# A long-convolution kernel: where two loads stand in the SyncE queue of an even step

## The chip, the cores and the metric

The kernel runs on one core of one Trainium2 chip. The metric is the device time of one execution in microseconds (us), as the median of several runs. A second source is one profiled execution, which gives every instruction of every engine with its start and its duration.

## The reference

Two blocks are computed one after the other, in float32. The first convolves 8 sequences of 5696 x 128 with one filter of the same length, by a Fourier transform of doubled length. The second is a soft mixture of experts over all 45568 resulting rows.

```python
Xf = np.fft.rfft(x, n=2 * S, axis=1)              # x: (8, 5696, 128)
Hf = np.fft.rfft(h, n=2 * S, axis=0)              # h: (5696, 128)
y = np.fft.irfft(Xf * Hf[None], n=2 * S, axis=1)[:, :S, :]
x = y.reshape(8 * 5696, 128)
logits = x @ phi                                  # 32 slots
d = softmax(logits, axis=0)                       # over the rows
slot_input = d.T @ x
slot_out = relu(slot_input @ w1[e]) @ w2[e]       # 4 slots for each of 8 experts
out = softmax(logits, axis=1) @ slot_out
```

## The kernel before, in words

The transform is split in two factors, N1 = 90 and N2 = 64, and is done for nine "batches": the filter h first (batch 0), then the eight sequences. The work of a batch is cut into 8 chunks (NJ = 8), and a hand-written loop over steps `t` (line 631) runs a software pipeline: one step starts one chunk of a batch, and later stages of earlier batches run in the same step. An even and an odd step make a pair. Nothing reorders the work: each engine does its instructions in the order in which the program writes them.

**The stages.** `stage_a(t, ...)` is the first factor (L241, TensorE), for the lower 60 of 90 frequencies in every step and for the upper 30 of two chunks in every odd step. ScalarE moves its result to `fst` (L243), and the SyncE queue stores it to the DRAM tensor `f` (L225): two stores of 240 KB for the lower frequencies, four of 120 KB for the upper ones. A batch's spectra are complete when its eight steps are over. They come back as tiles `gt`, one for each of 12 "units" of a batch, by `load_g` (L270, 512 KB). `stage_b1(u)` is the second factor on unit u and the product with the filter (L284 on TensorE into `bt`, L304 and L312 on VectorE). `stage_b2(u)` is the first factor of the inverse (L327 into `bz`); ScalarE moves it to `zst` (L332), and SyncE stores it: units 0 to 7 to `zm` in two stores of 256 KB, units 8 to 11 to `zr` in four stores of 128 KB (32 KB in the last unit). The frequencies in `zr` are z's last ones. `stage_c1(T)` is the last factor for a pair of chunks, T: matmuls L412 on `zc` (loaded from `zm`, `load_main`, L374, 1024 KB) and then L417 on `zx` (loaded from `zr`, `load_rest`, L385, 512 KB). It runs at the head of an odd step. All else (logits, the two softmaxes, the dispatch) follows on its result in later steps.

**Who does what where.** A step of a multiple of eight (t = 8, 16, ... 72) is the first in which a batch's spectra may be loaded. `prefetch(last)` issues `load_g` for units up to `last`, as far as their batch is stored. It is called from `slot_b` behind each `stage_b1(u)` with `u + AHEAD`, AHEAD = 3. There are three `gt` buffers, so `load_g(u)` can start when `stage_b1(u - 3)` is over. The first unit of a new batch is multiplied in the odd step that follows, behind `stage_c1`.

Steps t = 26, 34, ... 74 precede a new batch's first `stage_c1` (T = 0, 4, ... 24). In these the line `load_rest(pair(-1))` (L694) loads `zx` for that T. For the other three T of a batch, both loads stand together in an odd step, two steps ahead of their use (L680 to L682). There is a single pair of `zc` and `zx` buffers.

**The SyncE queue.** Nearly all transfers are issued by SyncE in program order. `pending` holds stores that are written down but not yet issued; `flush()` issues them. Each issue uses one of eight semaphores in turn, and first waits until the DMA that used it eight issues before has landed. `load_x` (L198) loads the input of a later chunk (768 KB).

In program order, an even step issues this on SyncE before the change:

| | t = 32, 40, ... 64 | t = 34, 42, ... 66 |
|---|---|---|
| 1 | `load_x` | `load_rest` (zx) |
| 2 | two stores of `f` | `load_x` |
| 3 | `load_g` of units 0 and 1 | two stores of `f` |
| 4 | stores of `zr` | `load_g` |
| 5 | `c_t`, `load_g` of unit 2, stores of `zr` | two stores of `zm` |
| 6 | | `c_t`, `load_g`, two stores of `zm` |

Of the kernel before, what the change touches and what calls it, by code (L numbers as in the profile page):

```python
# [70 lines left out]
def kernel(  # L71
# [34 lines left out]
    NJ = HALF // CH  # L106
# [6 lines left out]
    NQ = NJ // 2  # L113
# [95 lines left out]
    def fold(c):  # L209
        if c not in xs:  # L210
            return
        t_ = xs.pop(c)
        y_ = xf[c % len(xf)]
        i = CH * (c % 2)
        near, far = t_[:, 0, i:i + CH, :], t_[:, 1, ::-1, :][:, i:i + CH, :]
        for o in range(2):
            nc.gpsimd.tensor_tensor(out=y_[:, o, :, :], in0=near, in1=far,  # L217
                                    op=AL.subtract if o else AL.add)
        folded[c] = y_
# [3 lines left out]
    def flush():  # L223
        while pending:
            pending.pop(0)()  # L225
# [4 lines left out]
    def stage_a(c, high):  # L230

        g, j = divmod(c, NJ)
        st = apool.tile([P, CH, 2, D], F32, name="fst", tag="fst", bufs=4)
        if high:
            groups = [(c_, o, HALF, slice(HP, HP + HALF)) for c_ in (c - 1, c) for o in range(2)]
        else:
            groups = [(c, o, HP, slice(0, HP)) for o in range(2)]
        for q in range(2):
            p = bank()
            for i, (c_, o, m, cols) in enumerate(groups):  # L240
                nc.tensor.matmul(p[i * m:(i + 1) * m, :], s1[:, g // B, q + o, cols], columns(c_, o),  # L241
                                 start=True, stop=True)
            nc.scalar.activation(st[:, :, q, :],  # L243
                                 p[:, :].rearrange("p (n d) -> p n d", d=D), AF.Copy)
        k0, k1 = (LOW, N1) if high else (0, LOW)
        for i, (c_, o, m, _) in enumerate(groups):
            n0 = o * HALF + CH * (c_ % NJ)
            pending.append(partial(
                nc.sync.dma_start,
                out=fd[g][k0:k1, n0:n0 + CH, :, :].rearrange("k n c d -> k (n c d)"),  # L250
                in_=st[i * m:i * m + k1 - k0, :, :, :].rearrange("k n c d -> k (n c d)")))
        if high:
            for c_ in (c - 1, c):
                del folded[c_]
# [9 lines left out]
    def load_g(u):  # L264
        if u >= (B + 1) * NW:
            return
        g, w, us = parts(u)
        n = sum(k for _, k in us)
        t_ = bpool.tile([P, 4, 2, D], F32, name="gt", tag="gt", bufs=3)
        nc.sync.dma_start(  # L270
            out=t_[:, 0:n, :, :].rearrange("p q c d -> p q (c d)"),
            in_=fd[g][8 * w:8 * w + 2 * n].rearrange("(q a) r c d -> (a r) q (c d)", a=2))
        gs[u] = t_
# [42 lines left out]
    def stage_b2(u):  # L316
        g, w, us = parts(u)
        if g == 0:
            return
        m = len(us)  # L320
        y_ = prods.pop(u)
        bz = bps.tile([P, 2, 2, 2 * D], F32, name="bz", tag="bz")
        for o, (i, n) in enumerate(us):
            for q in range(n):
                r = slice(q * HP, (q + 1) * HP)
                for a in range(2):
                    nc.tensor.matmul(bz[a * HP:(a + 1) * HP, q, o, :], vt[r, i, a, :],  # L327
                                     y_[r, a * m + o, :, :].rearrange("p c d -> p (c d)"),
                                     start=True, stop=True)
        n = us[0][1]  # L330
        st = bpool.tile([P, 2, 2, 2 * D], F32, name="zst", tag="zst", bufs=3)
        nc.scalar.activation(st[:, 0:m, 0:n, :].rearrange("p o q x -> p q o x"),  # L332
                             bz[:, 0:n, 0:m, :], AF.Copy)
        k = m * n
        sv = st[:, :, :, :].rearrange("p o q x -> p (o q) x")
        for o in range(2):
            if 8 * w < MAIN:
                pending.append(partial(
                    nc.sync.dma_start,
                    out=zm[g - 1][o, 8 * w:8 * w + 2 * k].rearrange("(q a) r c d -> (a r) q (c d)", a=2),  # L340
                    in_=sv[o::2, 0:k, :]))
                continue
            k0 = 8 * w - MAIN
            for c in range(2):
                pending.append(partial(
                    nc.sync.dma_start,
                    out=zr[g % 2][o, c, k0:k0 + 2 * k].rearrange("(q a) r d -> (a r) q d", a=2),
                    in_=sv[o::2, 0:k, c * D:(c + 1) * D]))
# [30 lines left out]
    def load_rest(T):  # L379
        if T >= NT:  # L380
            return
        b, j = divmod(T, NQ)
        t_ = zs[T]
        n = 2 * CH
        nc.sync.dma_start(  # L385
            out=t_[1][:, :, :, :].rearrange("p h n d -> p (h n d)"),
            in_=zr[(b + 1) % 2].rearrange("o c k r d -> (o c k) r d")[:, j * n:(j + 1) * n].rearrange(
                "p r x -> p (r x)"))
# [214 lines left out]
    def units(t):  # L603
        g, i = divmod(t - LAG_B, NJ)
        if t < LAG_B or g > B:
            return []
        return [g * NW + k for k in range(sum(PER[:i]), sum(PER[:i + 1]))]
# [4 lines left out]
    AHEAD = 3  # L612
# [16 lines left out]
    wait_b2 = []  # L629

    for t in range(last_front + 1):
        us = list(units(t))

        def pair(lag):
            T, half = divmod(t - LAG_C - lag, 2)
            return T if half == 0 and 0 <= T < NT else None

        def prefetch(last):
            nonlocal loaded
            while loaded < len(queue) and queue[loaded][0] <= last \  # L640
                    and queue[loaded][0] // NW * NJ + NJ <= t:
                load_g(queue[loaded][0])
                loaded += 1

        def slot_b(due=True):
            fresh = due and bool(us)
            if fresh:
                u = us.pop(0)
                stage_b1(u)
                prefetch(u + AHEAD)  # L650
                wait_b2.append(u)
            if len(wait_b2) > fresh:
                stage_b2(wait_b2.pop(0))

        T, U, V, W, X = [pair(k) for k in (0, 2, 1, 3, 5)]
        if t < NA:
            stage_a(t, False)
            fold(t + 1)
        if t == last_front:
            assert T is None and U is None  # L660
            assert pair(-1) % NQ
            flush()
            dispatch(W)
            for i in range(3):
                slot_b()
                flush()
                if i == 1:
                    softmax_sum(W)
                    stage_c2(V)
            assert not us and not wait_b2  # L670
            stage_c6(X)
            stage_c3(V)
            column_max(V)
            break
        if t % 2:
            if T is not None:
                stage_c1(T)()
            flush()
            if pair(-2) is not None:
                load_main(pair(-2))  # L680
                if pair(-2) % NQ:
                    load_rest(pair(-2))  # L682
            slot_b()
            if U is not None:
                stage_c4(U)
            if t < NA:
                stage_a(t, True)
            if U is not None:
                stage_c5(U)
                softmax_exp(U)  # L690
            flush()
        else:
            if pair(-1) is not None and pair(-1) % NQ == 0:
                load_rest(pair(-1))  # L694
            if t < NA:
                load_x(t // 2 + 2)
            flush()
            if t == NJ:
                prefetch(AHEAD - 1)
            slot_b()  # L700
            if W is not None:
                softmax_sum(W)
                dispatch(W)
            flush()
            if V is not None:
                stage_c2(V)
            if X is not None:
                stage_c6(X)
            slot_b()
            if V is not None:  # L710
                stage_c3(V)
                column_max(V)
            flush()
        if t == NA:
            lead.close()
            wts = inner.enter_context(tc.tile_pool(name="wts", bufs=1, side="right"))
            w1s = wts.tile([P, E, F], F32, name="w1s")
        if NA < t <= NA + E:
            nc.sync.dma_start(out=w1s[:, t - NA - 1, :], in_=moe_w1[t - NA - 1])
# [213 lines left out]
```

## Time and profile before

| | |
|---|---|
| median of 3 runs | 912.35 us (912.24 to 916.9) |
| the profiled execution | 909.23 us, its span 907.4 us |
| mean granted TensorE clock | 0.903 |
| TensorE busy | 760.2 us (84% of the span) |
| VectorE, ScalarE, GpSimd busy | 601.4, 436.8, 399.8 us |
| DMA | 278.33 MB, mean 307 GB/s |

The profile's engines: PE is TensorE (matmuls), PEld its weight loads, DVE VectorE, ACT ScalarE, POOL GpSimd, SP SyncE, whose work is all issuing ("SPq"). "out<-in" names the tile written and the tiles read; L284 is line 284 of the kernel. Times count from the span's start. "PE bt L284 <- DMA gt<-f" reads: TensorE sat idle before the matmuls of L284 until a load of `gt` landed. When a DMA lands is seen from the trace's semaphore events, since each issue names its semaphore.

### The profile page before, as it was taken

How to read it: one execution, taken by the hardware profiler on the slowest of the kernel's cores; microseconds unless marked ns; L12 is line 12 of the kernel's file. 1: busy time of each engine (PE TensorE's matmuls, PEld its weight loads, DVE VectorE, ACT ScalarE, POOL GpSimd, SP SyncE). 2: the span in 40 equal slices, each digit the busy share in tenths (PEclk: the TensorE clock that was granted, in tenths of full speed). 3: DMA queues.
4: the chain of work that ended last, by engine and by line, in shares of the span. 5: the costliest groups of instructions: out<-in, count | busy, mean ns of one | idle time of the engine just before them, and what ended most of it. 6: DMA issues, size and time to landing. Idle time of an engine off the chain costs nothing.

```text
span 907.4 us, 21291 instructions
## 1 busy us (share of the span) xinstructions
PE 760.2 (84%) x8308; PEld 387.7 (43%) x8308; DVE 601.4 (66%) x896; ACT 436.8 (48%) x880; POOL 399.8 (44%) x353
## 2 busy tenths in 40 slices
PE   6857778689999989999998999799888877767893
PEld 2212233234444444444444444344444434344793
DVE  2029767568778867886877787678778766653552
ACT  2423234335556545665655655456544444563441
POOL 4634322444555655655655566456332224651000
PEclk9979889999999999999999999899988888766855
DMA  8989999999999999999999999999998768540798
GB/s 267 318 275 343 293 296 337 298 314 376 341 291 375 361 326 308 372 358 299 357 364 335 295 373 348 303 308 346 306 291 304 264 200 341 186 166 1 292 406 335
DMA packets 170443, 278.33 MB, mean 307 GB/s; under 512 B 13543, under 2 KB 128231, under 8 KB 165135
## 3 DMA queue, kind: packets, MB, share of 16 engines
q1 hardware_dynamic: 169336, 275.74, 89.7%
q10 hardware_dynamic: 1008, 1.25, 0.5%
q8 instruction: 66, 1.08, 0.5%
q14 instruction: 33, 0.27, 0.1%
HBM read 147.94 MB, written 129.00 MB: 305 GB/s over the span
## 4 chain that ended last, share of the span: by engine, by line
PE 47%; DMA 23%; ACT 8%; POOL 8%; DVE 6%; issue 6%; SPq 1%; ACTq 0%; DVEq 0%; POOLq 0%
PE bank L241 9%; DMA gt<-f 9%; PE bt L284 9%; PE bz L327 6%; POOL y L430 5%; PE bank L412 4%; DMA f<-fst 4%; PE op L886 3%; PE bank L439 3%; PE bank L417 3%; PE bank L448 2%; DMA zx<-zr 2%; ACT fst L243 2%; DMA out_dram<-o 2%; PE bank L527 2%
## 5 line engine op out<-in xcount | busy, mean ns | idle before, releaser
L241 PE MATMUL bank<-x,s 128*32 128x512 f32 (+1 forms) x1152 | 218.0, 620 | 12.9 <-POOL x L217 8.4
L217 POOL TENSOR_TENSOR x<-xc 128x512 f32<-128x512 f32 x144 | 180.4, 1278 | 107.2 <-PE bank L241 86.5
L284 PE MATMUL bt<-gt,wt 64*64 64x256 f32 x1620 | 125.0, 419 | 72.8 <-DMA gt<-f 33.0
L430 POOL TENSOR_TENSOR y<-y,op 128x512 f32<-128x512 f32 x64 | 77.6, 1213 | 206.8 <-DVE op L404 204.3
L304 DVE TENSOR_TENSOR pi<-bt,Hi 128x1024 f32<-128x1024 f32 x96 | 113.0, 1177 | 83.5 <-PE bt L284 83.3
L243 ACT ACTIVATE fst<-bank 128x512 f32<-128x512 f32 x216 | 122.8, 592 | 86.0 <-PE bank L241 57.7
L332 ACT ACTIVATE zst<-bz 128x1024 f32<-128x1024 f32 x96 | 93.3, 972 | 128.3 <-PE bz L327 109.4
L284 PEld LDWEIGHTS bt<-gt,wt 64*64 64x64 f32 x1620 | 58.3, 141 | 151.2 <-issue 79.1
L312 DVE TENSOR_TENSOR yf<-bt,pi 128x512 f32<-128x512 f32 x192 | 119.4, 663 | 3.3
L304 DVE TENSOR_TENSOR bt<-bt,Hr 128x1024 f32<-128x1024 f32 x96 | 113.0, 1177 | 0.0
L241 PEld LDWEIGHTS bank<-x,s 128*32 128x32 f32 (+1 forms) x1152 | 55.1, 126 | 129.8 <-issue 93.6
L327 PE MATMUL bz<-yf,vt 64*64 64x256 f32 x1440 | 110.4, 404 | 0.0
L327 PEld LDWEIGHTS bz<-yf,vt 64*64 64x64 f32 x1440 | 64.3, 143 | 25.5 <-issue 4.2
L512 POOL TENSOR_TENSOR L<-L,rs 128x512 f32<-128x512 f32 x32 | 33.5, 1048 | 91.6 <-DVE rs L511 66.4
L404 DVE TENSOR_TENSOR y<-bank,y 128x512 f32<-128x512 f32 x32 | 22.1, 692 | 76.7 <-ACT y L420 76.5
L439 PE MATMUL bank<-ident,y 109*128 109x109 f32 x512 | 62.7, 273 | 7.9 <-ACT yt L441 7.9
L504 ACT ACTIVATE L<-L 128x512 f32<-128x512 f32 x32 | 20.2, 630 | 94.7 <-POOL L L501 94.6
L430 POOL TENSOR_TENSOR y<-y,om 128x512 f32<-128x512 f32 x54 | 63.9, 1183 | 2.1
L439 PEld LDWEIGHTS bank<-ident,y 109*128 109x128 f32 x512 | 52.9, 149 | 19.4 <-POOL x L217 14.7
L412 PE MATMUL bank<-zc,im 64*64 64x512 f32 x480 | 60.8, 623 | 0.0
L441 ACT ACTIVATE yt<-bank 128x360 f32<-128x360 f32 x128 | 53.0, 482 | 7.7 <-PE bank L439 7.3
L420 ACT ACTIVATE y<-bank 128x512 f32<-128x512 f32 x32 | 19.1, 596 | 72.6 <-PE bank L417 72.6
(101 smaller groups left out, 862.5 us busy)
## 6 DMA issues: line engine op xcount, KB each, us to landing
gt<-f SPq DMA_DIRECT2D x99, 512.0 KB
f<-fst SPq DMA_DIRECT2D x144, 240.0 KB
zm<-zst SPq DMA_DIRECT2D x128, 256.0 KB
zc<-zm SPq DMA_DIRECT2D x30, 1024.0 KB
xc<-in_x_dram SPq DMA_DIRECT2D x32, 768.0 KB
f<-fst SPq DMA_DIRECT2D x144, 120.0 KB
out_dram<-o SPq DMA_DIRECT2D x16, 1024.0 KB
zx<-zr SPq DMA_DIRECT2D x30, 512.0 KB
```

Source lines behind the costliest of these rows:

```text
L217: nc.gpsimd.tensor_tensor(out=y_[:, o, :, :], in0=near, in1=far, op=AL.subtract if o else AL.add)
L241: nc.tensor.matmul(p[i * m:(i + 1) * m, :], s1[:, g // B, q + o, cols], columns(c_, o), start=True, stop=True)
L243: nc.scalar.activation(st[:, :, q, :], p[:, :].rearrange("p (n d) -> p n d", d=D), AF.Copy)
L284: nc.tensor.matmul(bt[q * HP:(q + 1) * HP, a, o, :], wt[r, 2 * i + q, :], t_[r, 2 * o + q, :, :].rearrange("p c d -> p (c d)"), start=True ...
L304: nc.vector.tensor_tensor(out=p_, in0=pv, in1=h_, op=AL.mult)
L312: nc.vector.tensor_tensor(out=y_[r, 0:k, c, :], in0=pv[:, :, c, :], in1=pi[r, 0:k, 1 - c, :], op=op_)
L327: nc.tensor.matmul(bz[a * HP:(a + 1) * HP, q, o, :], vt[r, i, a, :], y_[r, a * m + o, :, :].rearrange("p c d -> p (c d)"), start=True, sto ...
L332: nc.scalar.activation(st[:, 0:m, 0:n, :].rearrange("p o q x -> p q o x"), bz[:, 0:n, 0:m, :], AF.Copy)
L412: nc.tensor.matmul(ps[o, c][h_ * HP:(h_ + 1) * HP, :], im[r, c, :], zt[r, h_, :, c, :], start=True, stop=False)
L430: eng.tensor_tensor(out=part_, in0=part(v, 0), in1=o_[:, :, :], op=sign)
L439: nc.tensor.transpose(p[:, i * TR:(i + 1) * TR], ys[T][0:TR, k * CH + i, 0:D], ident[0:TR, 0:TR])
L441: nc.scalar.activation(yt[:, k * CH:(k + 1) * CH, :, :], of_tokens(p), AF.Copy)
```

## The change

In steps that are a multiple of 8, `prefetch` is called at the head of the step, ahead of `load_x` and of the stores of `f`. From t = 16 on, its limit is three units above the last multiplied one, so that it issues the new batch's first unit alone; unit 1 stays where it was. At t = 8, it issues units 0, 1 and 2. In steps 26, 34, ... 74, `load_rest` leaves the head of the step and stands behind the first `slot_b` and a `flush()`, hence behind `load_x`, the stores of `f`, the first `load_g` and the first two stores of `zm`.

```diff
         else:
-            if pair(-1) is not None and pair(-1) % NQ == 0:
-                load_rest(pair(-1))
+            if t % NJ == 0:
+                prefetch(wait_b2[-1] + AHEAD if wait_b2 else AHEAD - 1)
             if t < NA:
                 load_x(t // 2 + 2)
             flush()
-            if t == NJ:
-                prefetch(AHEAD - 1)
             slot_b()
+            if pair(-1) is not None and pair(-1) % NQ == 0:
+                flush()
+                load_rest(pair(-1))
             if W is not None:
                 softmax_sum(W)
                 dispatch(W)
```

## The prediction

> **What bounds the kernel now.** I read the page first, then the waits, the chain of waits, and the timeline at the two places that the change touches.
>
> ```profile
> span 907.4 us, 21291 instructions
> PE 760.2 (84%) x8308; PEld 387.7 (43%) x8308; DVE 601.4 (66%) x896; ACT 436.8 (48%) x880; POOL 399.8 (44%) x353
> ```
>
> PE is the busiest engine. In the middle of the span it is nearly the only bound: in the PE timeline the first-factor matmuls of odd steps start at 265.67, 285.82 and 305.97, so a pair of steps takes 20.15 us, and PE's gaps in two such pairs sum to 1.5 us. What PE loses there is lost to the span. The waits tell to whom it loses most:
>
> ```profile
> PE bt L284 <- DMA gt<-f: 33.0, 10, 10.2
> ```
>
> Eight of these ten are the first unit of a new batch: 10.2 us at t = 9, then 5.2, 3.1, 0.5, 3.4, 2.1, 1.7 and 5.5 at t = 17, 25, ... 65, and none at 73; together 31.6. The chain of waits shows the largest of the middle, and the other place that the change touches:
>
> ```profile
> 506.52 5.35 DMA zr<-zst
> 511.94 4.60 DMA zx<-zr
> 516.59 1.19 PE bank L417 x16
> ...
> 575.05 8.04 DMA gt<-f
> 583.22 1.99 PE bt L284 x16
> ```
>
> The columns are start and length. A load of `gt` is issued at 575.05, takes 8.04 us, and PE starts 0.1 us after it lands. But `zx` also lands at 516.54, and L417 starts at 516.59: that load has no slack. The SyncE timeline of step 34 shows what stands behind it:
>
> ```profile
> 265.26 0.35 SPq L385 DMA_DIRECT2D zx<-zr  x1
> 265.66 0.76 SPq L198 DMA_DIRECT2D xc<-in_x_dram  x1
> 266.46 0.88 SPq L225 DMA_DIRECT2D f<-fst  x2
> 267.44 0.41 SPq L270 DMA_DIRECT2D gt<-f  x1
> 267.95 1.83 SPq L225 DMA_DIRECT2D zm<-zst  x2
> ```
>
> and the PE timeline what waits for it:
>
> ```profile
> 267.53 1.95 PE L412 MATMUL bank<-zc,im 64*64 64x512 f32 x16
> 269.41 1.11 PE L417 MATMUL bank<-zx,ir 26*64 26x512 f32 x16
> ```
>
> By the semaphore events, this `zx` landed at 269.20, 3.9 us after its issue and 0.2 us before its use. The `gt` load issued two microseconds later landed at 274.98 (7.5 us), the second `zm` store at 276.28 (7.2 us). Most DMAs of this stretch land in the order of issue, about 1.4 us apart for 512 KB: they queue, and what stands ahead in the queue sets the landing.
>
> **Part 1, the first spectra.** Nothing is added or removed; one `load_g` (three at t = 8) passes `load_x` and two stores of `f`. At t = 32, `load_x` is issued at 242.00 and `gt` at 243.51, so the issue moves up 1.5 us. For the landing the bytes that it passes count. 512 KB of `gt` take 1.4 us between landings, so 768 KB of `load_x` take about 2.1, an estimate from that; the two stores of `f` land 0.6 to 0.7 us apart each. So the load lands some 3.4 us earlier. At t = 8 and 16 it cannot be issued earlier: it follows the lower stores of `f` of the step before, which land at 49.23 and 97.84, just when the load is issued now; but the transfers that it passes are still behind it, so I count the same there. The bound of this from below is nothing. Each wait shrinks by what it has, up to 3.4: 3.4 + 3.4 + 3.1 + 0.5 + 3.4 + 2.1 + 1.7 + 3.4 = 21.0 us. If the queue is also shorter by then, all but the 10.2 and the 5.2 go completely, 23.1.
>
> What was passed comes later: `load_x` and `f` by the time of one `gt`, 1.4 us. `load_x` feeds a fold three steps (30 us) later, and the stores of `f` are read eight steps on, so both are covered. ScalarE waits for a store of `fst` only in the first 105 us (27.6 us, 11 times); past that its four buffers cover the 1.4. At t = 8 three loads pass and stand waiting until 49.23, which puts `load_x` and `f` some 6 us back; PE's own 10.2 us wait hides that, and uncovered it would eat the 3.4. Unit 1 is next: at t = 32 it lands at 252.13 and is multiplied at 257.45, so it has 5 us of slack.
>
> **Part 2, z's last frequencies.** `load_rest` passes behind `load_x`, two `f`, one `gt` and two `zm`: 768 + 480 + 512 + 512 = 2272 KB on SyncE's only queue. It issues no new DMA. It adds a wait: SyncE now has to see the `zst` of that slot ready before `zx` goes; at t = 34 the two `zm` are issued at 267.95 with `zst` evicted at about 261.7, so that wait is covered. Taken away is SyncE's stop at the head of the step until the `zr` stores have landed, 0.2 to 0.8 us, with which `load_x` waited.
>
> Where will `zx` land? From above: the same seven transfers have to move, so it lands when the last of them does now. Those landings are 197.68, 276.28, 360.23, 442.13, 524.52, 609.75 and 681.62 for t = 26, 34, ... 74; L417 starts now at 190.13, 269.41, 353.20, 435.75, 516.59, 602.76 and 682.45. The differences are 7.6, 6.9, 7.0, 6.4, 7.9, 7.0 and none: 42.8 us. From below: issued when the second `zm` has been, less its own 0.4 us at the head, and taking only what it takes now at the head, 3.9 to 4.9 us; that gives 3.6, 3.9, 2.7, 2.5, 3.8 and 3.2, together 19.7. Nearest are `gt` and `zm` at that place in the queue, with 7.2 to 7.7 us, so I take the upper end, less the stop that is removed and the issue of `zx` itself (0.75 us in each of six): 38.3.
>
> L417 sits at the head of the odd step, and PE is in order: behind it are L284, L327 and the next first factor; ScalarE waits for it with the eviction (L420), then VectorE and GpSimd (L430). So PE stands still for the whole wait.
>
> The Trainium skill would make this smaller: "DMA: Bandwidth & Descriptors", in its section on the anatomy of one DMA, gives a fixed 2.0 us plus bytes over 436 GB/s (fitted on another issue path), which for 512 KB is an estimate of 3.2 us from issue to landing. By it, `zx` issued at 269.4 would land at 272.6, and the six waits would be some 3 us each and the whole change near zero. The 7.5 us of `gt` in the same place speaks against it here, since that rule knows no queue.
>
> **The clock.** A long wait costs more than itself. The windows view of the 5.5 us wait and after it, with PE's busy time first and the granted clock, DMA share and GB/s last:
>
> ```profile
> 577.71:583.22 5.51, 0.00 (x0) 0.03 (x1) 2.67 (x4) 1.09 (x2) 2.66 (x3) 0.74 1.05 358
> 583.22:587.00 3.78, 3.78 (x24) 2.09 (x24) 1.74 (x2) 0.38 (x1) 2.00 (x2) 0.50 1.03 334
> ```
>
> After it PE ran at half clock for 3.8 us. The eight steps with it (odd step 59 to 67, 512.56 to 599.02) took 86.5 us, against 80.5 for those with the 1.7 us wait (51 to 59): 5.9 more for 3.8 more of wait, so the clock cost 2.1. The same for the waits of 3.4 and 2.1 us (83.8 and 82.5 us) gives 1.6 each. Six new long waits at 2.1 are 12.6; those at t = 17, 41, 49 and 65 that shorten or go give back 1.6 x 3 + 2.1 = 6.9. Net +5.7 us. "TensorE: Matmul & The Clock Gate", on oscillation, puts the limit at PE idle for more than about 3.4 us; here 2.1 us sufficed at 416.4 (0.53 granted after it), 1.7 at 498.6 did not (1.00).
>
> **The sum.** 38.3 + 5.7 - 21.0 = +23 us. Against the profiled execution, 909.2 (907.4 of span and 1.8 around it), that is 932. The median of the runs lies 3.1 above that execution: 935.
>
> **The rivals.**
>
> *The saved waits do not count.* Between a batch's first unit and its `zx` there are ten microseconds. If the DMA queue does not move up with PE, PE reaches L417 earlier and waits longer for the same landing. Then the savings of t = 25 to 65 (14.2 us) are lost, and +37 remains, with the upper end of part 2 +42: 949 to 954. For it: DMA is at 358 and 334 GB/s around 583. Against it: SyncE waits for PE and ScalarE in the steps between, so its stream moves with them.
>
> *The load is cheap behind the stores.* `zx` takes what it takes now: 19.7, at most 6 x 1.6 - 6.9 = 2.7 for the clock, less 21 to 23: -3 to +1; with anything up to half way to the main case, 909 to 922. For it: at 264 to 267 the queue runs almost dry (115 to 143 GB/s), and it has been given 7 us of slack once PE has waited. Against: the 7.5 us of `gt` in that place.
>
> *Faster.* The place is the front of SyncE's step 34. Its last two upper `f` stores wait for ring slots until 262.74 and 264.52. If a shorter queue frees these, `load_x` can go at the end of its fold, 261.6 instead of 265.66; `zx` then lands 4.1 us earlier than my 275.5 (276.28 less 0.75), 271.4, or 2.0 us behind L417's start. Six of these make 12; less 23, and with no change from the clock, -11 us: 901. It decides if a wait for `zx` falls below 21 / 6 = 3.5 us. Against: that late slot comes from the `zc` and `gt` of step 33, issued with no backlog of SyncE (254.15, waiting for ScalarE), so it should return whatever went before.
>
> That the change does nothing for the first spectra, because their load waits for the stores of `f`, holds for the issue at t = 8 and 16 alone; everywhere it would be 38.3 + 5.7 = +44, at the upper end.
>
> **How the numbers follow.** Main case 0.52 (+10 to +33), savings lost 0.22, cheap load 0.18 (0.08 of it within 4.6 us, 0.5%, about what a measurement can tell), faster 0.08. So slower 0.84, same 0.08, faster 0.08. Range: from the cheap load, 910, to the lost savings with the upper end, 955; the main case alone 922 to 945.
>
> **What would show it.** In the changed profile, "PE bt L284 <- DMA gt<-f" should fall from 33 to about 12 us, nearly all at t = 9 and 17. "PE bank L417 <- DMA zx<-zr" should rise from a few to about 38, in six waits of 5 to 8 us, at t = 27, 35, ... 67, with half clock behind each, and none at t = 75. `zx` in step 34 should be issued behind the second `zm` and land 6 to 7 us after L412 ends. I am wrong if those waits are under 3.5 us each, or if first-unit waits stay.

## The result and the profile after

The changed kernel takes 937.78 us (median, 934.83 to 939.17) against 912.3 us in the same comparison: a ratio of 1.0272 with a 95% interval of 1.0219 to 1.0325. The forecast was 935 (910 to 955), slower. The profiled execution after took 939.17 us, 29.9 more than the one of before. Ratios here and below are of fast executions; one of the ten executions of the kernel *g_only* (below), 3743.59 us, is left out of its ratio, and the record does not say what slowed it.

The head of the page says that the work of the engines is the same and only the span grew:

```profile
span 937.4 us, 21285 instructions
PE 763.5 (81%) x8308; PEld 383.2 (41%) x8308; DVE 601.1 (64%) x896; ACT 436.3 (47%) x880; POOL 399.8 (43%) x353
```

The waits, with idle time in us, how often, and the longest:

```profile
PE bank L417 <- DMA zx<-zr: 45.1, 6, 10.0
PE bt L284 <- DMA gt<-f: 12.0, 6, 6.5
```

Before, the first of them read:

```profile
PE bank L417 <- DMA zx<-zr: 2.5, 2, 2.3
```

Both lines moved as foretold: L417 from 2.5 to 45.1 us in six waits, L284 from 33.0 to 12.0. Step 34 shows how one of the six arises, first on SyncE (start, length, the store or load issued) and then on TensorE:

```profile
267.57 0.33 SPq L198 DMA_DIRECT2D xc<-in_x_dram  x1
268.01 0.83 SPq L225 DMA_DIRECT2D f<-fst  x2
268.93 0.60 SPq L270 DMA_DIRECT2D gt<-f  x1
269.62 2.31 SPq L225 DMA_DIRECT2D zm<-zst  x2
271.99 0.66 SPq L385 DMA_DIRECT2D zx<-zr  x1
```

```profile
268.77 1.95 PE L412 MATMUL bank<-zc,im 64*64 64x512 f32 x16
278.30 2.02 PE L417 MATMUL bank<-zx,ir 26*64 26x512 f32 x16 [7.58 <-DMA zx<-zr]
```

`zx` is now issued behind six transfers of its own step, 1.3 us after TensorE has done L412 (270.72), and takes 6.27 us. That piece is now a link of the chain that ended last:

```profile
271.99 6.27 DMA zx<-zr
278.30 2.02 PE bank L417 x16
```

The windows show the stop, and that the clock answers to it (TensorE's busy time first; the last three columns are the granted clock, the DMA share and GB/s):

```profile
270.72:278.30 7.58, 0.00 (x2) 0.00 (x1) 0.00 (x0) 0.00 (x0) 0.00 (x0) 0.83 1.02 358
278.30:282.60 4.30, 4.30 (x40) 1.79 (x44) 1.57 (x3) 1.08 (x2) 0.00 (x0) 0.50 1.09 411
282.60:290.00 7.40, 7.40 (x80) 3.05 (x72) 5.95 (x8) 4.63 (x10) 6.72 (x6) 1.00 0.98 366
```

For 7.6 us none of the five engines computes, while DMA runs at 358 GB/s; then TensorE works 4.3 us at half clock. Behind each of the six waits, the clock granted over the next 3.9 to 4.3 us was 0.50 to 0.59.

### The profile page after: what moved, and what is told of

The parts are those of the page before. It is cut to its first block, busy times and chain, and to the rows that moved or that the text cites. A ratio compares the mean times of both kernels' runs of the same rounds, so it can differ in the third digit from the quotient of the medians.

```text
span 937.4 us, 21285 instructions
## 1 busy us (share of the span) xinstructions
PE 763.5 (81%) x8308; PEld 383.2 (41%) x8308; DVE 601.1 (64%) x896; ACT 436.3 (47%) x880; POOL 399.8 (43%) x353
## 4 chain that ended last, share of the span: by engine, by line
PE 46%; DMA 26%; ACT 8%; DVE 6%; issue 6%; POOL 4%; SPq 3%; ACTq 0%; DVEq 0%; POOLq 0%
PE bank L241 10%; PE bt L284 9%; PE bz L327 7%; DMA gt<-f 6%; DMA zx<-zr 6%; PE bank L412 4%; DMA out_dram<-o 4%; PE bank L417 4%; DMA f<-fst 3%; PE bank L439 3%; POOL y L430 3%; PE bank L448 2%; DMA zr<-zst 2%; ACT fst L243 2%; SPq L225 2%
## 5 line engine op out<-in xcount | busy, mean ns | idle before, releaser
L284 PE MATMUL bt<-gt,wt 64*64 64x256 f32 x1620 | 125.5, 420 | 53.6 <-issue 28.1
L284 PEld LDWEIGHTS bt<-gt,wt 64*64 64x64 f32 x1620 | 58.4, 142 | 137.1 <-issue 76.9
L417 PE MATMUL bank<-zx,ir 26*64 26x512 f32 x480 | 39.2, 714 | 45.1 <-DMA zx<-zr 45.1
L420 ACT ACTIVATE y<-bank 128x512 f32<-128x512 f32 x32 | 19.1, 596 | 120.9 <-PE bank L417 120.9
L439 PEld LDWEIGHTS bank<-ident,y 109*128 109x128 f32 x512 | 53.3, 150 | 18.8 <-POOL x L217 13.9
L412 PE MATMUL bank<-zc,im 64*64 64x512 f32 x480 | 60.8, 623 | 0.0
```

What stands on the lines that cost most here:

```text
L284: nc.tensor.matmul(bt[q * HP:(q + 1) * HP, a, o, :], wt[r, 2 * i + q, :], t_[r, 2 * o + q, :, :].rearrange("p c d -> p (c d)"), start=True ...
L412: nc.tensor.matmul(ps[o, c][h_ * HP:(h_ + 1) * HP, :], im[r, c, :], zt[r, h_, :, c, :], start=True, stop=False)
L417: nc.tensor.matmul(p[h_ * HP:(h_ + 1) * HP, :], ir[r, :], zx[r, h_, :, :], start=False, stop=True)
L439: nc.tensor.transpose(p[:, i * TR:(i + 1) * TR], ys[T][0:TR, k * CH + i, 0:D], ident[0:TR, 0:TR])
```

## The experiments

My theory was the sum on record: part 1 is worth about -21 us of waits, part 2 about +38, each by itself. The chief rival was that waits saved at the first unit are handed on to `zx`. Each ratio below is to the kernel before, run beside that kernel.

### Each part alone, and `zx` at places between

*g_only* has part 1 alone; *z_only* has part 2 alone, with `prefetch` where it was. *z_after_x* and *z_after_g* have part 1, and `load_rest` at two places between the head and the changed one. The sketch lists the calls of an even step; `prefetch` runs in steps 8, 16, ... and `load_rest` in steps 26, 34, ...:

```
 even step, by kernel:           g_only      z_after_x   z_after_g   changed
     load_rest (head)            here
     prefetch (t % NJ == 0)      x           x           x           x
     load_x                      x           x           x           x
     load_rest                               here
     flush(): two stores of f    x           x           x           x
     slot_b(): load_g, zm noted  x           x           x           x
     load_rest                                           here
     flush(): two stores of zm   x           x           x           x
     load_rest                                                       here
```

> The first spectra of a new batch at the head of the step, zx left at the head too (first of all). Theory (position in the queue, the two parts add): TensorE's waits for the first units fall from 33 to about 12 us as in the changed kernel, zx keeps its place and its landing moves up with the rest; the time falls by the 21 us and some 5 of half clock, to 884 to 893 us. Rival (saved waits are eaten): the landing of zx stays where it is, L417 waits for it instead in six odd steps, together 10 to 20 us, and the time is 903 to 912 us.

> zx behind x, f, the first load of gt and two stores of zm; the first spectra left where they were. Theory (the two parts add): six waits at L417 of 6 to 7.5 us, and the first-unit waits stay near 33 us; 958 to 968 us. Rival (the wait at L417 gives the queue 7 us of lead, with which the first-unit waits go by themselves): from t = 33 on no first-unit wait is left, waits for gt fall to about 20 us, L417 waits for 40 to 48 us; 938 to 950 us, and then most of the 21 us saved in the changed kernel were not due to its first part.

> First spectra at the head, and zx behind the load of x alone. Theory (bytes ahead in the queue): zx lands the time of 768 KB, about 2.1 us, and one issue, 0.4 us, later than at the head of the step, so six waits at L417 are 2 to 3 us longer than with zx at the head; 12 to 20 us above the kernel with the first spectra alone moved. Rival (SyncE is held up by the zm stores, which wait for their data): nothing ahead of zx waits for data, so no new wait, within 4 us of the kernel with the first spectra alone moved.

> First spectra at the head, and zx behind x, the two stores of f and the load of gt, but ahead of the two zm stores. Theory (bytes ahead in the queue): 1760 KB or about 4.8 us ahead, six waits at L417 of 4.5 to 6 us, 1.3 us each less than in the changed kernel; 925 to 932 us. Rival (the zm stores' wait for their data): about the time of the kernel with zx behind x alone.

Measured, with the two waits of each profile ("PE bt L284 <- DMA gt<-f" and "PE bank L417 <- DMA zx<-zr"); the row of the changed kernel is from its own comparison, with 912.3 us before:

| kernel | median us | ratio (95%) | L284 | L417 | sum |
|---|---|---|---|---|---|
| before | 913.39 | 1 | 33.0 | 2.5 | 35.5 |
| g_only | 911.05 | 0.9974 (0.9942 to 1.0006) | 6.3 | 21.8 | 28.1 |
| z_after_x | 911.62 | 0.9975 (0.9944 to 1.0007) | 16.3 | 19.1 | 35.4 |
| z_after_g | 930.22 | 1.0192 (1.0145 to 1.024) | 15.5 | 32.4 | 47.9 |
| changed | 937.78 | 1.0272 (1.0219 to 1.0325) | 12.0 | 45.1 | 57.1 |
| z_only | 947.04 | 1.0378 (1.0331 to 1.0425) | 19.0 | 42.6 | 61.6 |

In g_only the wait at t = 9 is put down to the store that the load follows, 6.2 us more, which makes its sum 34.3:

```profile
PE bank L417 <- DMA zx<-zr: 21.8, 6, 5.3
PE bt L284 <- DMA gt<-f: 6.3, 5, 2.0
PE bt L284 <- DMA f<-fst: 6.2, 1, 6.2
```

So **part 1 alone does not save 21 us but 2.3, and the interval of its ratio includes 1.** The rival is right here: 33 us of waits at L284 became 12.5, and 2.5 at L417 became 21.8. The timelines of g_only at step 34 show the exchange:

```profile
260.71 1.95 PE L412 MATMUL bank<-zc,im 64*64 64x512 f32 x16
267.21 2.01 PE L417 MATMUL bank<-zx,ir 26*64 26x512 f32 x16 [4.55 <-DMA zx<-zr]
```

```profile
254.75 2.14 SPq L225 DMA_DIRECT2D zr<-zst  x3
256.99 4.28 SPq L225 DMA_DIRECT2D f<-fst  x4
263.19 0.35 SPq L385 DMA_DIRECT2D zx<-zr  x1
```

TensorE has L412 done at 262.66 where before it was at 269.48: 6.8 us earlier. `zx` goes at 263.19 where it went at 265.26, only 2.1 us earlier, since it waits for the last store of `zr`, and that one stands at the end of a queue that has not become shorter:

```profile
256.30 6.84 DMA zr<-zst
263.19 3.98 DMA zx<-zr
267.21 2.01 PE bank L417 x16
```

From the issue of the new batch's first `gt` to that of `zx`, for the first six batches that have both, SyncE took 21.1 to 22.0 us for 23 or 24 transfers before, 21.9 to 25.1 for 26 or 27 in g_only, 25.4 to 30.9 for 32 or 33 in the changed kernel: 0.79 to 0.94 us each. An earlier `gt` starts this stretch earlier, with three more transfers in it; its end is where TensorE now waits.

**Part 2 alone costs 33.7 us**, and on top of part 1 27 (911.05 to 937.78). The rival in the expectation of z_only came true, in the time (938 to 950) and in the waits. Its six waits are 6.0 to 7.8 us:

```profile
PE bank L417 <- DMA zx<-zr: 42.6, 6, 7.8
```

Its first-unit waits stayed at 9.9 and 5.5 us at t = 9 and 17, and fell to at most 1.7 afterwards, with no load of `gt` moved. From issue to landing these loads took 7.1 to 8.6 us, no less than before (7.1 to 8.1); but from t = 25 to 65 they were issued 6.4 to 7.1 us ahead of the time at which TensorE was ready for them, before 2.7 to 6.9. While TensorE stands at L417, SyncE gets ahead. Part 1 on top of part 2 is worth 9 us (947.04 to 937.78), most of it at t = 9 and 17, where no `zx` wait has come before.

*z_after_x* missed its theory (12 to 20 us above g_only) and came within the 4 us of its rival: behind `load_x`, the load of `zx` costs nothing. Its SyncE timeline says why:

```profile
257.99 4.28 SPq L225 DMA_DIRECT2D f<-fst  x4
262.37 1.31 SPq L198 DMA_DIRECT2D xc<-in_x_dram  x1
263.79 0.36 SPq L385 DMA_DIRECT2D zx<-zr  x1
```

With `zx` at the head, in g_only, SyncE stood idle from 261.27 to 263.19 for the landing of `zr`; `load_x` fits into that time, and `zx` is issued 0.6 us later than in g_only. It then takes 6.1 to 6.6 us instead of 4.0 to 5.1 (once 6.6), but the L417 waits are no longer, and from one new batch's first L417 to the next the kernel takes 83.8 us, g_only 84.8 (means of the first four such stretches). *z_after_g* came in the time that its theory named (925 to 932): behind two stores of `f` and a `gt` the six waits are 3.5 to 6.3 us, each 0.6 to 3.8 us shorter than with the `zm` stores in front. Its rival, that only the `zm` stores' wait for their data matters, is out: no `zm` stands ahead of `zx` here. The step from "behind x" to "behind x, f and gt" is the dear one, 18.6 (911.62 to 930.22) of the 27 us.

The theory counted bytes ahead in the queue, and the landings bear that out: behind other transfers of its step, `zx` lands 1.1 to 1.4 us after the one just in front of it. The column on `load_x` counts from its issue, the others show how the wait at L417 comes about (means of the six, in us):

| kernel | KB passed | issue of `load_x` to landing of `zx` | `zx`, issue to landing | issued ahead of L412's end | wait at L417 |
|---|---|---|---|---|---|
| g_only | 0 | | 4.9 | 1.3 | 3.6 |
| z_after_x | 768 | 7.0 | 6.4 | 3.2 | 3.2 |
| z_after_g | 1760 | 10.1 | 7.8 | 2.5 | 5.4 |
| changed | 2272 | 11.2 | 6.6 | -0.9 | 7.5 |

So more in front means a later landing, but not a longer time from issue to landing: behind the `zm` stores `zx` is itself issued later, when part of the queue has gone.

### What sets the stretch: the `zr` stores elsewhere

If SyncE's stretch up to `zx` is the bound, taking the `zr` stores off SyncE should let part 1 win. *zr_act* is the kernel before with these issued by ScalarE behind the eviction; *g_zr_act* and *after_zr_act* are the same with part 1 and with both parts.

```diff
-                pending.append(partial(
-                    nc.sync.dma_start,
+                nc.scalar.dma_start(
                     out=zr[g % 2][o, c, k0:k0 + 2 * k].rearrange("(q a) r d -> (a r) q d", a=2),
-                    in_=sv[o::2, 0:k, c * D:(c + 1) * D]))
+                    in_=sv[o::2, 0:k, c * D:(c + 1) * D])
```

> The kernel before, with the stores of z's last frequencies (zr) issued by ScalarE behind its eviction instead of by SyncE; order of the rest unchanged. From the first load of a batch's spectra to the issue of zx SyncE takes 21.1 to 22.0 us for 24 DMAs in every batch, 12 of them zr stores. Theory (SyncE's issuing and its ring of eight slots set this stretch): without the 12 it shrinks to 17 to 19 us, the waits for gt and zx together fall from 35 to 15 to 25 us, and the time to 892 to 902 us. Rival (the bytes on the DMA engines set it): the stretch stays at 21 to 22 us and the time within 4 us of before.

> The first spectra at the head of the step (zx at the head too), and the zr stores issued by ScalarE. Theory (SyncE's issuing sets the stretch up to zx, which is why moving the first spectra alone only handed the wait on to zx): now the saved waits count; waits for gt and zx together 10 to 20 us, 884 to 898 us, and 5 to 10 us below the kernel with the zr stores moved alone. Rival (bytes on the DMA engines): as the first spectra moved alone, 905 to 912 us.

> The changed kernel with the zr stores issued by ScalarE. Theory (zx is late by the DMAs that stand ahead of it, zr stores among them): zx is issued 3 to 5 us earlier in the stretch, the six waits at L417 fall from 45 to 20 to 30 us, 915 to 925 us. Rival (only the transfers that it was moved behind count, and the bytes): 935 to 940 us as the changed kernel.

Measured: 1009.1 us (1.1044, 1.0983 to 1.1105), 973.29 (1.0663, 1.0598 to 1.0728) and 990.38 (1.0833, 1.0768 to 1.0898). No theory expected this, and it does not answer the question, because a new cost buries it. ScalarE's and SyncE's timelines of zr_act:

```profile
272.08 2.60 ACTq L345 DMA_DIRECT2D zr<-zst  x4
```

```profile
261.45 7.12 SPq L225 DMA_DIRECT2D f<-fst  x3
274.35 0.33 SPq L198 DMA_DIRECT2D xc<-in_x_dram  x1
```

In this trace the issues of both engines take the same eight completion semaphores in turn, in program order. So SyncE's `load_x` waits until 274.29, when a `zr` store that ScalarE issued has landed, and SyncE issues nothing from 268.57 to 274.35. The largest line of this kind in SyncE's waits is

```profile
SPq L225 <- DMA zr<-zst: 58.5, 12, 7.9
```

The other way round this trace has no such wait: whenever a `zr` store of ScalarE took a semaphore that SyncE had used, that transfer had landed at least 2.8 us earlier. But the four issues take ScalarE 2.6 us a unit, and its evictions stand behind them. The L284 waits went to 59.6 us:

```profile
PE bt L284 <- DMA gt<-f: 59.6, 12, 11.6
```

Part 1 did help here (1009.1 to 973.29): g_zr_act has 15.8 us left at L284 (and 6.9 at t = 9 put down to a store of `f`), and 4.2 us at the matmuls on `zx` (L416 there). That would fit a `zx` with slack, but with SyncE held up by ScalarE's stores it proves nothing for the kernel in question.

The next try keeps SyncE as the only queue and halves the number of `zr` stores: *zr_wide* stores both parts of a value together, two stores of 256 KB instead of four of 128 KB, with `zr`, `zx` and the table `ir` laid out to match, and `zx` loaded in two halves.

```diff
-            for c in range(2):
-                pending.append(partial(
-                    nc.sync.dma_start,
-                    out=zr[g % 2][o, c, k0:k0 + 2 * k].rearrange("(q a) r d -> (a r) q d", a=2),
-                    in_=sv[o::2, 0:k, c * D:(c + 1) * D]))
+            pending.append(partial(
+                nc.sync.dma_start,
+                out=zr[g % 2][o, k0:k0 + 2 * k].rearrange("(q a) r c d -> (a r) q (c d)", a=2),
+                in_=sv[o::2, 0:k, :]))
...
-                r = slice((2 * o + c) * HALF, (2 * o + c) * HALF + N1 - MAIN)
-                nc.tensor.matmul(p[h_ * HP:(h_ + 1) * HP, :], ir[r, :], zx[r, h_, :, :],
+                r = slice((2 * h_ + o) * HALF, (2 * h_ + o) * HALF + N1 - MAIN)
+                nc.tensor.matmul(p[h_ * HP:(h_ + 1) * HP, :], ir[r, c, :], zx[r, :, c, :],
```

> The kernel before, with z's last frequencies stored as z's first ones are: two stores of 256 KB a unit instead of four of 128 KB, the same bytes (zx is then loaded in two halves of 256 KB). From the first load of a batch's spectra to the issue of zx there are 18 DMAs instead of 24, 305 GB/s over 21.5 us before. Theory (SyncE's stream, some 0.9 us for each DMA, sets this stretch): it shrinks to 16 to 19 us, the waits for gt and zx together fall from 35 to 15 to 25 us, and the time to 892 to 902 us. Rival (the bytes on the DMA engines set it): 21 to 22 us as before, and the time within 4 us of before.

> The first spectra at the head of the step, zx at the head too, and z's last frequencies in half as many stores. Theory (SyncE's stream up to zx handed the saved waits on): with the stream shorter the first spectra's gain is kept, 884 to 896 us and 4 to 10 us below the kernel with the wider stores alone. Rival (bytes on the DMA engines): no faster than the wider stores alone, 900 to 912 us.

> The changed kernel with z's last frequencies in half as many stores. Theory (zx is late by its place in SyncE's stream): 27 DMAs instead of 33 ahead of zx in the stretch, zx 3 to 5 us earlier, six waits at L417 of 20 to 28 us together instead of 45, 912 to 922 us. Rival (only the transfers that zx was moved behind count): 934 to 940 us.

Measured: 932.53 us (1.0227, 1.0178 to 1.0276), 931.51 (1.0206, 1.0131 to 1.028) and 950.1 (1.0422, 1.0367 to 1.0476). All three are above both ranges that were expected. The stretch of zr_wide did shrink from the second of these batches on, to 18.8 to 19.6 us for 19 transfers, and no matmul of TensorE waits for `zx` any more. That is 0.99 to 1.03 us for each transfer, so the stretch does not go by their number alone. The waits for `gt` are 27.2 us, which is more than the 15 to 25 expected for both. And the matmuls on `zx` became slower, in the lines by form (busy us, mean ns):

```profile
L419 PE MATMUL bank<-zx,ir 26*64 26x512 f32 x480 | 59.7, 600 | 0.0
```

They are the matmuls of this line of before:

```profile
L417 PE MATMUL bank<-zx,ir 26*64 26x512 f32 x480 | 33.8, 619 | 2.5 <-DMA zx<-zr 2.5
```

Now they are busy 25.9 us more, which is enough to cover the 20 lost. So I tried to get their speed back: *zr_wide4* and, with part 1, *g_zr_wide4* order them so that four different groups of rows follow one another (a matmul here reads 26 partitions that start at 0, 32, 64 or 96: its row group).

```diff
-        for h_ in range(2):
-            for (o, c), p in ps.items():
+        for half in (list(ps.items())[:2], list(ps.items())[2:]):
+            for h_ in range(2):
+                for (o, c), p in half:
```

> The wider zr stores, with the order before the change, and the zx matmuls reordered so that four different row groups follow one another, as in the kernel before (in the first wide kernel two groups followed one another, and its 16 matmuls of a pair took 1.96 us instead of 1.11: 32 x 0.85 = 27 us). Theory (SyncE's stream sets the stretch up to zx): the 27 us go and the shorter stretch stays, 18.8 to 19.6 us instead of 21.5; 900 to 908 us. Rival (bytes on the DMA engines; the stretch was short only because TensorE was slower): the stretch returns to 21 to 22 us, 908 to 914 us.

> As that, and with the first spectra at the head of the step. Theory (with the shorter stream the first spectra's gain is kept): 4 to 10 us below the kernel without that move, 893 to 902 us, no wait of over 2 us at L417. Rival (the queue is full either way and the saved waits go elsewhere): within 4 us of the kernel without that move.

Measured: 923.09 us (1.0107, 1.0063 to 1.015) and 924.8 (1.01, 1.0057 to 1.0144). The first is above both ranges; the second came as its rival said. The order did not bring the speed of these matmuls back:

```profile
279.01 1.95 PE L420 MATMUL bank<-zx,ir 26*64 26x512 f32 x16
```

With 1.11 us for these sixteen before, this is as slow as in zr_wide. Yet the kernel lost only 9.3 us for 25.2 us of added matmul time (59.0 less 33.8). The idle time of TensorE did not pay for that: it is 147 to 148 us in the profiles of before, zr_wide and zr_wide4 alike. TensorE's busy time rose by only 13.8 us (760.2 to 774.0), as its other matmuls were shorter, at a granted clock of 0.923 instead of 0.903. So the shorter stretch took no idle time away.

Part 1 gains nothing here either, neither with the first wide layout (-1.0 us) nor with the second (+1.7). It is not `zx` that takes the gain this time. From zr_wide4 to g_zr_wide4 the waits for `gt` fell from 36.8 to 25.0 us, those for `zx` rose from none to 5.0, and TensorE's idle time fell from 147.7 to 137.4 us; but its matmuls were busy 14.6 us longer, at a granted clock of 0.914 instead of 0.923. Why is not shown.

What bounds a batch beneath the visible waits is left open: SyncE's time for each issue, the landing of `zr` before `zx`, and the DMA engines are not told apart. For the last of them speaks the DMA share, the last column but one, in this line of the kernel before, over the four batches from L417 at 269.4 to L417 at 602.8:

```profile
269.40:602.80 333.40, 311.45 (x3562) 149.97 (x3559) 252.41 (x384) 189.41 (x384) 188.10 (x160) 0.98 1.00 337
```

and by the same four batches of the changed kernel, 20.7 us longer with the DMA share down to 0.96:

```profile
278.30:632.40 354.10, 315.72 (x3552) 150.17 (x3552) 252.15 (x384) 189.05 (x384) 188.12 (x160) 0.96 0.96 318
```

The share is of time in which the DMA engines have work, not of their best rate: behind the wait shown above they moved 411 GB/s, here 337. TensorE is idle for 22 of the 333.4 us before the change, so a load order can win little more than that in these batches. No version beat the kernel before by more than the measurement can tell; g_only and z_after_x equal it.

## Why the prediction was right, and where its sum was not

**The total and the mechanism of part 2 held.** 932 was foretold for the profiled execution, which took 939.17, and 935 for the median, which is 937.78. `zx` at the end of a queue of 2272 KB makes L417 wait six times, with half clock behind, and not at t = 75: there `zx` landed at 710.68 and L417 came to it at 712.18. z_only shows by itself that this is the cause.

**Term of part 2: foretold 38.3, measured 45.1.** The six waits are 10.0, 7.6, 5.7, 7.9, 7.0 and 6.9 us. I took the landing of the last transfer and the start of L417 from the trace of before, both at their old places: 42.8 us. z_only, with the waits at t = 9 and 17 still there, has 42.6, so of the 4.5 us that I took off for the stop at the head and the issue of `zx` nothing is seen. The other 2.5 come with part 1, most of them in the first wait (10.0 us, in z_only 6.0): with the saved waits L417 comes earlier relative to the queue. In step 34 the working had `zx` issued just before the end of L412; it was issued 1.3 us behind it, and landed 7.5 us after that end, not 6 to 7. That what stands ahead in the queue sets the landing held: in all six, `zx` landed 1.2 to 1.3 us behind the second `zm`.

**Term of part 1: foretold -21.0, measured -21.0 in the wait line, but not as part 1's own.** This is the step that failed behind a right number. At t = 9 and 17 the working fits: 10.2 and 5.2 less 3.4 would be 6.8 and 1.8, and the profile has 6.55 and 2.36. The load itself also comes sooner: from issue to landing, the first `gt` of t = 17 to 65 took 7.1 to 8.1 us before and 4.2 to 5.4 after. From t = 25 on all first-unit waits went to zero, and I put those 14.2 us down to the earlier issue. z_only shows that part 2's own waits remove most of them with no load moved, and g_only shows that the earlier issue alone turns them into waits for `zx`. That the sum came right all the same is in part luck: where the working has 21 us of saved waits for part 1, part 1 alone gained 2.3 us and on top of part 2 9, and part 2 alone cost 33.7. The rival "the saved waits do not count" described part 1 alone rightly. My reason against it, that SyncE's stream moves with the engines, was wrong in size: at step 34 of g_only TensorE moved up by 6.8 us, and `zx` by 2.1.

**Term of the clock: foretold +5.7, about +7.6 in the trace.** Step 71 starts 31.2 us later than before, of which 2.0 us were there by step 8. Waits at L417 account for 42.6 more, at L284 for 21.0 less; 29.2 - 42.6 + 21.0 leaves 7.6 us for half-clock stretches and all else. The prediction gave two waits, 1.7 us without half clock behind it and 2.1 with it. Their length alone does not decide: before the change the wait of 3.1 us at t = 25 (168.92 to 172.03) was followed by 3.8 us at a granted clock of 1.00.

**The cheap load** fell clearly: behind the stores `zx` took over 6 us from issue to landing, not the 3.9 to 4.9 of the head. The Trainium skill's fixed time plus bytes over bandwidth ("DMA: Bandwidth & Descriptors", the anatomy of one DMA) gave an estimate of 3.2 us; it is fitted on another issue path, and the measured 6.27 us decides against using it in a full queue. **Faster** fell with it: its condition was waits under 3.5 us at L417, and the least is 5.7.

## What to carry to other kernels

When TensorE waits for the first load of a phase and the same queue later delivers another load just in time, price both as one chain: here a wait removed at the first was paid at the second. That a shorter stretch between them would keep the gain is not shown: in the wide layout the stretch was shorter and the waits fell, but the time did not. For the second load, count the bytes that it lets pass from the issue of the first of them, and set the landing against the time at which the engine will come. A load needed within one step must not stand behind stores that nobody reads for several steps, but, as z_after_x shows, it may stand behind a transfer that fills time in which the queue would wait anyway. Run each half of a change alone, even when the total comes out as foretold: here a right total hid that one term belonged to the other part.

## What the runs showed of the hardware that I had not expected

- In these programs, issues from ScalarE and from SyncE shared eight completion semaphores in program order, so SyncE waited for the landings of ScalarE's stores (58.5 us in one line of zr_act); with the `zr` stores on ScalarE the kernel took 1009.1 us instead of 911.57.
- On the one queue of SyncE, a 512 KB load of `zx` behind other transfers of its step landed 1.1 to 1.4 us after the one just in front of it, in all 18 cases of z_after_x, z_after_g and the changed kernel, 6.1 to 8.7 us after its own issue.
- Sixteen 26-row matmuls took 1.11 us when each value's parts lay in row groups of their own, and 1.95 to 1.96 us in the wide layout, whether or not four row groups followed one another. Why is open. Before, the four row groups that follow one another write four PSUM banks; in zr_wide two groups alternate, and in zr_wide4 four groups write two banks, two groups to a bank in different halves of its partitions. No run tells these apart.
